# One load queue, wider squares, smaller key-value tiles and fewer last stores in a polysketch-attention and squared-ReLU kernel

## The chip, the cores and the metric

The kernel runs on one core of a Trainium2 chip. The time is the device time in microseconds of one launch. A profiled execution of the same program gives the views that are quoted here. The engines are named as in the profile: PE (TensorE, matrix multiplication; PEld is its weight loading), DVE (VectorE), ACT (ScalarE), POOL (GpSimd) and SP (SyncE, which here only issues DMAs). All DMAs run on the core's 16 DMA engines, through queues that SP, ACT and POOL fill.

## What is computed

Four batches with four heads each have 1088 positions of q, k and v with 32 elements. A feature map takes two 8-element sketches of a row and multiplies them out to 64 features. The attention is linear in these features, and its output (4352 rows of 128) goes through a feed-forward layer whose activation is the square of a ReLU:

```python
def phi(x):
    a = einsum('rd,bhsd->bhsr', S1, x)
    b = einsum('rd,bhsd->bhsr', S2, x)
    return einsum('bhsi,bhsj->bhsij', a, b).reshape(..., 64)
q_p, k_p = phi(q), phi(k)
kv = einsum('bhsf,bhsd->bhfd', k_p, v)
z = sum(k_p, axis=2)
x = (q_p @ kv) / (q_p @ z + 1e-6)      # (4352, 128), heads side by side
out = square(maximum(x @ w_in, 0)) @ w_out     # 128 -> 2048 -> 128
```

Inputs and output are float32. The feed-forward part is computed in bfloat16, the attention in float32.

## The kernel before

**Loads.** `load(b)` (L87) fetches one batch: k as one transfer of 544 KB into `k_in`, v as four transfers of 128 KB (one for each head) and two of 16 KB (the last two of every 34 positions) into `v_in`, and q as one transfer of 544 KB into `q_in`. For batch 0, v is issued by ACT (L102) and k and q by SP, behind two small loads of the sketch matrices into `S12` (L77, L78). SP then issues batches 1 to 3. The framework numbers the hardware-queue DMAs of SP and ACT round eight lanes, and a DMA waits until the one before it in its lane has landed, so at most eight are under way. POOL issues the two weight loads, `w_out` and `w_in` (L121, L119: float32 in memory, converted to bfloat16 on the way), after a copy of one element (L118) that waits for q of batch 0.

**Keys.** `k_stage(b)` (L160) makes the key-value matrix of one batch. DVE transposes k in 32x32 blocks (`block_transpose`, L146) into `kT`. PE projects it onto both sketches (L176). For each of two halves of the positions (`gi` is 0 and 1), ACT copies one sketch out of PSUM into `ka` (L191), DVE multiplies the two sketches out to `kp` in two instructions of 512 columns (L193, one for each half `f` of the features), and v is copied into `v_pad`, which has a column of ones behind each head's 32 columns (L202, L204; by ACT for batch 0, by POOL for the others). PE sums `kp` times `v_pad` over the positions (L215). One matmul takes two heads: 64 columns of `kp` as weights and 66 columns of `v_pad`, so half of the result is the product of one head's keys with the other head's values and is not used. Each half has its own PSUM tile. DVE copies the first half's sums to `kvc` (L226) and adds the second half's with four instructions, one for each head (L230), into `KV`, whose other blocks are zero.

**Queries.** Nine chunks (`ci`): two of 512 columns for each batch, and one of 256 with the last two of every 34 positions of all batches (`qT_rem`). `q_feat` (L254) projects (L266, float32, 128x512), and DVE transposes (L272), multiplies out (L274) and transposes back (L282) to `qp`. `q_out` (L289) multiplies `qp` by `KV` (L304), divides by the denominators on DVE (L318 to L321) and transposes the result on PE (L330), and ACT copies it to `xT` (L336).

**Feed-forward.** `f_stage` (L349) goes over 16 blocks of 128 hidden columns, two at a time: two matmuls into `h_ps` (L358), a ReLU on ACT into `r_sb` (L362, 128x1024), the square on DVE into `g_sb` (L364, 128x1024), and 8 matmuls into `o_ps` (L370). ACT copies `o_ps` to `osb` (L380), and SP stores it: four transfers of 64 KB for a chunk (L383), and for the ninth chunk eight of 16 KB (L389), one for each batch and each of the last two positions.

**Order.** A prologue emits batch 0's keys and chunk 0's queries. After it the feed-forward of one chunk is interleaved with the attention of later ones: each `yield` of `f_stage` advances the attention by some steps (L418 to L432). The Tile framework places each engine's instructions, by a schedule of its own; instructions under `pin` keep the program's order, and `chain` does that for a list of matmuls. Each engine runs its instructions strictly in that order.

Of the kernel before, what the change touches and what calls it, by code (L numbers as in the profile page):

```python
# [21 lines left out]
def kernel(  # L22
# [52 lines left out]

    S12 = consts.tile([2 * r, H, D], F32)
    nc.sync.dma_start(out=S12[:r, 0, :], in_=S1)  # L77
    nc.sync.dma_start(out=S12[r:, 0, :], in_=S2)  # L78

    kin_t, qin_t, vraw, vpad = {}, {}, {}, {}  # L80
    for b in range(B):
        kin_t[b] = kin.tile([128, NJ, D], F32, tag=f"k{b}", name="k_in")
        qin_t[b] = kin.tile([128, NJ, D], F32, tag=f"q{b}", name="q_in")
        vraw[b] = vin.tile([128, H, NLO + 1, D], F32, tag=f"v{b}", name="v_in")
        vpad[b] = vin.tile([128, H, NLO + 1, VW], F32, tag=f"vp{b}", name="v_pad")

    def load(b, veng):  # L87
        nc.sync.dma_start(out=kin_t[b], in_=k[b].rearrange("h (t j) d -> (h t) j d", j=NJ))
        for h in range(H):
            vr = v[b, h].rearrange("(t j) d -> t j d", j=NJ)[:, : 4 * NLO, :]  # L90
            veng.dma_start(
                out=vraw[b][:, h, :NLO, :],
                in_=vr.rearrange("t (i l) d -> i t (l d)", i=4),
            )
        for j2 in range(2):
            veng.dma_start(
# [5 lines left out]
    load(0, nc.scalar)  # L102
    for b in range(1, B):
        load(b, nc.sync)


    ident = consts.tile([128, 128], F32)
    make_identity(nc, ident)
    ident_b = consts.tile([128, 128], BF16)
    nc.vector.tensor_copy(ident_b, ident)  # L110
    for b in range(B):
        nc.gpsimd.memset(vpad[b][:, :, :, D:VW], 1.0)
# [4 lines left out]
    w_in_sb = consts.tile([128, C_TILES, 128], BF16)  # L117
    nc.gpsimd.tensor_copy(w_in_sb[:1, 0, :1], qin_t[0][:1, 0, :1])  # L118
    nc.gpsimd.dma_start(out=w_in_sb, in_=moe_w_in.rearrange("d (ct c) -> d ct c", c=128))  # L119
    w_out_sb = consts.tile([128, C_TILES, 128], BF16)  # L120
    nc.gpsimd.dma_start(out=w_out_sb, in_=moe_w_out.rearrange("(ct c) d -> c ct d", c=128))  # L121

# [23 lines left out]
    def block_transpose(dst, dst_rem, src):  # L146
# [6 lines left out]
        pin(  # L153
            nc.vector.transpose(
                dst_rem, src[:, 4 * NLO :, :].rearrange("p j d -> p (j d)")
            )
        )


    def k_stage(b):  # L160

        kt = kTp.tile([128, S], F32, tag="kT", name="kT")
        block_transpose(kt[:, :1024], kt[:, 1024:], kin_t.pop(b))
# [21 lines left out]
        def features(gi):  # L185
            kk = kks[gi]
            ka = kab_pool.tile([128, 5 * H, r], F32, tag="ka", name="ka")
            kps[gi] = kp = kp_pool.tile([128, 2, 5 * H, 4, r], F32, tag="kp", name="kp")
            for P, g0, g1 in ((128, 0, 4 * H), (64, 4 * H, 5 * H))[: gi + 1]:
                kabv = kk[:P, g0 * 2 * r : g1 * 2 * r].rearrange("p (g x) -> p g x", x=2 * r)  # L190
                nc.scalar.copy(ka[:P, g0:g1], kabv[:, :, :r])  # L191
                for f in range(2):
                    nc.vector.tensor_tensor(  # L193
                        out=kp[:P, f, g0:g1],
                        in0=ka[:P, g0:g1, f * 4 : f * 4 + 4, None].to_broadcast(
                            [P, g1 - g0, 4, r]
                        ),
                        in1=kabv[:, :, None, r:].to_broadcast([P, g1 - g0, 4, r]),
                        op=ALU.mult,
                    )  # L200
# [5 lines left out]
        kvc = kab_pool.tile([128, 2, 2, VW], F32, tag="kvc", name="kvc")  # L206

        def sums(gi):
            kk, kp, seq = kks[gi], kps[gi], seqs[gi]
            kv = kk[:, KV0 : KV0 + 4 * VW].rearrange("p (f x w) -> p f x w", f=2, x=2)  # L210
            for m, P in tiles[gi]:
                for f in range(2):
                    for g in range(2):
                        seq.append(
                            nc.tensor.matmul(  # L215
                                kv[64 * g : 64 * g + 64, f],
                                kp[:P, f, m * H + 2 * g : m * H + 2 * g + 2].rearrange(
                                    "p g i j -> p (g i j)"
                                ),
                                vt[:P, 2 * g : 2 * g + 2, 4 * gi + m, :],  # L220
                                start=(m == 0 and f == 0),
                                stop=(m == len(tiles[gi]) - 1 and f == 1),
                            )
                        )
            if gi == 0:
                nc.vector.tensor_copy(kvc, kv)  # L226
            else:
                for h in range(H):
                    rows = slice(32 * h, 32 * h + 32)
                    nc.vector.tensor_tensor(  # L230
                        out=KV[rows, b, :, h % 2, :],
                        in0=kvc[rows, :, h % 2],
                        in1=kv[rows, :, h % 2],
                        op=ALU.add,
                    )
# [9 lines left out]
    def q_load_stage(b):  # L245
        qt = kTp.tile([128, 1024], F32, tag="qT", name="qT")
        block_transpose(qt, qT_rem[:, b], qin_t.pop(b))
# [101 lines left out]
    def f_stage(ci):  # L349
# [5 lines left out]
        for g2 in range(C_TILES // 2):  # L355
            h_ps = ps_h.tile([128, 2, 512], F32, tag="h", name="h_ps")
            for u in range(2):
                nc.tensor.matmul(  # L358
                    h_ps[:, u, :N], w_in_sb[:, 2 * g2 + u, :], xT[:, :N], start=True, stop=True
                )  # L360
            rt = r_pool.tile([128, 2, 512], BF16, tag="r", name="r_sb")
            nc.scalar.activation(rt[:, :, :N], h_ps[:, :, :N], ACTF.Relu)  # L362
            gt = g_pool.tile([128, 2, 512], BF16, tag="g", name="g_sb")
            nc.vector.tensor_mul(gt[:, :, :N], rt[:, :, :N], rt[:, :, :N])  # L364
            yield
            for u in range(2):
                ct = 2 * g2 + u
# [16 lines left out]
        else:  # L384
            for m in range(2):
                for g in range(4):
                    b, j2 = 2 * m + g // 2, g % 2
                    o = out[b * S : (b + 1) * S].rearrange("(t j) d -> j t d", j=NJ)
                    nc.sync.dma_start(  # L389
                        out=o[32 + j2], in_=osb[32 * g : 32 * (g + 1), m, :]  # L390
# [72 lines left out]
```

## Time and profile before

| what | value |
|---|---|
| time, median of 3 runs | 151.01 us (150.84 to 151.1) |
| profiled execution | 150.13 us, of which 148.3 us are the span of the profile |
| PE, DVE, ACT, POOL busy | 110.3, 108.1, 80.1, 9.1 us |
| k of batch 0 transposed from | 6.30 us |
| last head of v of batch 0 landed | 15.2 us |
| first matmul of the feed-forward | 28.6 us |
| weight loads: issued, us until landed | `w_out` 8.36, 15.1; `w_in` 9.65, 16.2 |
| last instruction of the attention's DVE part (`xb` of chunk 8) | ends at 125.2 us |
| last copy of `o_ps` on ACT (L380) | 142.07 to 142.44 us |

How to read it: a row of the groups names the line, the engine, the operation, and the tile written and read, with its shape and count; then the busy time in us and the mean duration of one in ns; then the idle time of the engine before these instructions and what ended most of it. A float32 matmul leaves two records. A line of the chain is a start in us, a duration in us, and the engine and line. A line of the waits is the instruction that waited, the one that released it, the sum in us, how often, and the longest. A row of a stretch gives its length and then, for PE, PEld, DVE, ACT and POOL in this order, the busy us and the number of instructions, and last the granted clock of PE, the mean number of busy DMA queues per engine, and GB/s. A busy PE is modelled from matmuls in a pipeline, and some matmul records can be missing.

### The profile page before, as it was taken

The page shows a single profiled execution, that of the slowest core. Times are in us where ns is not written, and L with a number is a line of the kernel's source. Part 1 is how long each engine was busy: PE and PEld are TensorE (multiplying, and loading weights), DVE is VectorE, ACT ScalarE, POOL GpSimd, SP SyncE. Part 2 cuts the span into 40 slices and gives each one's busy share as a digit, 9 for nine tenths or more (in the row PEclk, how much of TensorE's full clock was granted, in tenths as well). Part 3 has the DMA queues.
Part 4 walks back from the last instruction along what each step waited for, and adds up shares of the span by engine and source line. Part 5 has one row for each costly group of instructions (what it writes and reads, how often), then busy time and mean ns, then how long its engine had stood idle before and what let it go on. Part 6 is the DMA issues. An engine that isn't in the chain of part 4 may idle for free.

```text
span 148.3 us, 4011 instructions
## 1 busy us (share of the span) xinstructions
PE 110.3 (74%) x1693; PEld 73.7 (50%) x1709; DVE 108.1 (73%) x225; ACT 80.1 (54%) x107; POOL 9.1 (6%) x22
## 2 busy tenths in 40 slices
PE   0050764879997897797988797998897988999820
PEld 0050633437854773584636473764462755566510
DVE  2362476399999859976998986987996987666510
ACT  4000400296664429476294639565837758999810
POOL 2050001104007000000000000000000000000000
PEclk9999999599999689999999999999999999999995
DMA  3949892294452000110002002000200030020201
GB/s 73 358 136 213 160 279 64 102 260 137 121 175 76 23 0 0 39 43 0 0 0 74 1 4 71 4 0 7 66 5 4 0 74 1 0 75 0 73 13 24
DMA packets 8594, 10.22 MB, mean 69 GB/s; under 512 B 4096, under 2 KB 6400, under 8 KB 8576
## 3 DMA queue, kind: packets, MB, share of 16 engines
q1 hardware_dynamic: 5552, 8.36, 19.4%
q0 software_dynamic: 2208, 1.05, 5.4%
q10 hardware_dynamic: 816, 0.56, 1.3%
q8 instruction: 13, 0.21, 0.6%
q14 instruction: 5, 0.04, 0.1%
HBM read 8.78 MB, written 2.23 MB: 74 GB/s over the span
## 4 chain that ended last, share of the span: by engine, by line
DVE 40%; PE 29%; ACT 12%; DMA 8%; issue 5%; ACTq 1%
DVE g_sb L364 14%; ACT r_sb L362 10%; DMA v_in<-in_v_dram 8%; PE kab_ps L215 7%; PE o_ps L370 6%; DVE qf L274 6%; PE pr_ps L266 6%; DVE qp L282 5%; PE nd_ps L304 4%; DVE ab L272 3%; PE h_ps L358 3%; DVE kp L193 3%; DVE xb L321 2%; PE xT_ps L330 2%; DVE KV L230 2%
## 5 line engine op out<-in xcount | busy, mean ns | idle before, releaser
L362 ACT ACTIVATE r_sb<-h_ps 128x1024 bf16<-128x1024 f32 (+1 forms) x72 | 66.9, 984 | 21.0 <-PE pr_ps L266 6.7
L364 DVE TENSOR_TENSOR g_sb<-r_sb 128x1024 bf16<-128x1024 bf16 (+1 forms) x72 | 45.9, 656 | 9.8 <-ACT r_sb L362 9.4
L358 PE MATMUL h_ps<-xT,w_in_sb 128*128 128x512 bf16 (+1 forms) x128 | 37.7, 367 | 8.2 <-ACT r_sb L362 6.3
L370 PE MATMUL o_ps<-w_out_sb,g_sb 128*128 128x128 bf16 x544 | 40.8, 223 | 3.2 <-DVE g_sb L364 1.9
L370 PEld LDWEIGHTS <-g_sb 128*128 128x128 bf16 x544 | 32.3, 99 | 18.3 <-DVE g_sb L364 14.0
L358 PEld LDWEIGHTS <-w_in_sb 128*128 128x128 bf16 x144 | 12.7, 99 | 16.7 <-issue 12.5
L215 PE MATMUL kab_ps<-v_pad,kp 128*64 128x66 f32 (+1 forms) x288 | 11.7, 234 | 7.1 <-ACT v_pad L202 5.8
L193 DVE TENSOR_TENSOR kp<-ka,kab_ps 128x512 f32<-128x512 f32 (+1 forms) x24 | 12.0, 543 | 6.2 <-ACT ka L191 6.2
L215 PEld LDWEIGHTS kab_ps<-v_pad,kp 128*64 128x64 f32 (+1 forms) x288 | 10.3, 145 | 11.1 <-ACT v_pad L202 6.0
L336 ACT COPY xT<-xT_ps 128x512 bf16<-128x512 bf16 (+1 forms) x9 | 5.1, 563 | 17.7 <-PE xT_ps L330 17.7
L304 PEld LDWEIGHTS nd_ps<-KV,qp 64*64 64x64 f32 x544 | 9.7, 142 | 6.3 <-DVE qp L282 4.7
L304 PE MATMUL nd_ps<-KV,qp 64*64 64x66 f32 x544 | 11.3, 231 | 1.4 <-DVE KV L230 1.2
L272 DVE STREAM_TRANSPOSE ab<-pr_ps 128x512 f32<-128x512 f32 (+1 forms) x9 | 6.2, 685 | 8.5 <-PE pr_ps L266 8.5
L274 DVE TENSOR_TENSOR qf<-ab 128x1024 f32<-128x1024 f32 (+1 forms) x9 | 10.7, 1185 | 0.2
L266 PE MATMUL pr_ps<-qT,Wq 128*128 128x512 f32 x16 | 10.2, 721 | 0.7 <-DVE qT L148 0.7
L282 DVE STREAM_TRANSPOSE qp<-qf 128x1024 f32<-128x1024 f32 (+1 forms) x9 | 10.6, 1179 | 0.1
L380 ACT COPY osb<-o_ps 128x512 f32<-128x512 f32 (+1 forms) x9 | 5.1, 570 | 7.4 <-PE o_ps L370 7.4
L176 PE MATMUL kab_ps<-Wk,kT 128*64 128x64 f32 x136 | 6.4, 249 | 3.3 <-DVE Wk L131 3.3
L176 PEld LDWEIGHTS kab_ps<-Wk,kT 128*64 128x64 f32 x136 | 5.5, 159 | 4.6 <-DVE Wk L131 3.4
L191 ACT COPY ka<-kab_ps 128x128 f32<-128x128 f32 (+1 forms) x12 | 2.9, 240 | 8.4 <-PE kab_ps L176 7.0
L321 DVE TENSOR_TENSOR xb<-nd_ps,rec 128x256 bf16<-128x256 f32 (+1 forms) x18 | 6.6, 405 | 0.0
L202 POOL COPY v_pad<-v_in 128x512 f32<-128x512 f32 x6 | 4.5, 779 | 31.7 <-DMA v_in<-in_v_dram 31.7
(39 smaller groups left out, 40.8 us busy)
## 6 DMA issues: line engine op xcount, KB each, us to landing
k_in<-in_k_dram SPq DMA_DIRECT2D x4, 544.0 KB
q_in<-in_q_dram SPq DMA_DIRECT2D x4, 544.0 KB
out_dram<-osb SPq DMA_DIRECT2D x32, 64.0 KB
v_in<-in_v_dram SPq DMA_DIRECT2D x12, 128.0 KB
v_in<-in_v_dram ACTq DMA_DIRECT2D x4, 128.0 KB
w_out_sb<-in_moe_w_out_dram POOLq DMA_DIRECT2D x1, 512.0 KB, 15.1
w_in_sb<-in_moe_w_in_dram POOLq DMA_DIRECT2D x1, 512.0 KB, 16.2
out_dram<-osb SPq DMA_DIRECT2D x8, 16.0 KB
```

Of the source, the lines that this page charges most:

```text
L176: nc.tensor.matmul(kk[64 * c : 64 * c + 64, m * 64 : (m + 1) * 64], kt[:, c0 + 64 * c : c0 + 64 * c + 64], Wk.rearrange("p h x -> p (h x)" ...
L193: nc.vector.tensor_tensor(out=kp[:P, f, g0:g1], in0=ka[:P, g0:g1, f * 4 : f * 4 + 4, None].to_broadcast([P, g1 - g0, 4, r]), in1=kabv[:, : ...
L215: nc.tensor.matmul(kv[64 * g : 64 * g + 64, f], kp[:P, f, m * H + 2 * g : m * H + 2 * g + 2].rearrange("p g i j -> p (g i j)"), vt[:P, 2 * ...
L266: nc.tensor.matmul(pr[:, :N], Wq.rearrange("p h x -> p (h x)"), cols, start=True, stop=True)
L272: nc.vector.transpose(ab[:, :nj].rearrange("p j x -> p (j x)"), pr[:, :N])
L274: nc.vector.tensor_tensor(out=qf[:, :nj], in0=ab[:, :nj, :r, None].to_broadcast([128, nj, r, r]), in1=ab[:, :nj, None, r : 2 * r].to_broad ...
L282: nc.vector.transpose(qp[:, :, :N].rearrange("p f (j t) -> p j f t", t=32), qf[:, :nj].rearrange("p j (f i) k -> p j f (i k)", f=2),)
L304: nc.tensor.matmul(nds[g][64 * c : 64 * c + 64, m * 2 * VW : (m + 1) * 2 * VW], qp[rows, f, c0 : c0 + 64], KV[rows, bs[2 * m + c], f].rear ...
L358: nc.tensor.matmul(h_ps[:, u, :N], w_in_sb[:, 2 * g2 + u, :], xT[:, :N], start=True, stop=True)
L362: nc.scalar.activation(rt[:, :, :N], h_ps[:, :, :N], ACTF.Relu)
L364: nc.vector.tensor_mul(gt[:, :, :N], rt[:, :, :N], rt[:, :, :N])
L370: nc.tensor.matmul(o_ps[:, m, :], gt[:, u, m * 128 : (m + 1) * 128], w_out_sb[:, ct, :], start=(ct == 0 and m == 0), stop=(ct == C_TILES - ...
```

## The change

Four things, in the words of the diff below (helper lines that only move are left out).

- **Loads.** The identity matrix is built first. The sketch matrices are loaded by ACT. All of k, v and q are issued by SP: for each batch k, v, q. POOL's one-element copy ahead of the weight loads waits for the last head of v of batch 0 instead of q of batch 0, and a second one-element copy writes into `k_in` of batch 1 from `w_in`, so that the load of k of batch 1 waits for the weights. In the program as built, SP's order is k, v, q of batch 0; v, q of batch 1; k of batch 2; k of batch 1; then v, q of batch 2 and all of batch 3.
- **Squares.** `r_sb` and `g_sb` hold four blocks instead of two. ACT fills `r_sb` with two ReLUs of 128x1024 as before, DVE squares 128x2048 in one instruction, and 16 matmuls into `o_ps` follow. The pools still have three buffers each.
- **Key-value sums.** `kp` is multiplied out by one instruction of 1024 columns (one of 64x256 for the remainder). A matmul takes one head: 32 columns of `kp` as weights and 33 columns of `v_pad`, into 32 rows of the result. Both halves of the positions add up in the PSUM tile of the first half, and `kvc` and the adds are gone. For batch 0, ACT and DVE copy two heads each into `KV`, in turns (in the built program each of the four waits for the one before). For the other batches ACT copies the whole result to `kvs` (128x66) and POOL copies the four heads (32x66) into `KV`.
- **Last rows.** `qT_rem` is ordered by position first, so that 64 rows of `osb` are one batch. The ninth chunk is stored by four transfers of 64 rows, two issued by SP and two by ACT.

```diff
+    ident = consts.tile([128, 128], F32)
+    make_identity(nc, ident)
     S12 = consts.tile([2 * r, H, D], F32)
-    nc.sync.dma_start(out=S12[:r, 0, :], in_=S1)
-    nc.sync.dma_start(out=S12[r:, 0, :], in_=S2)
+    nc.scalar.dma_start(out=S12[:r, 0, :], in_=S1)
+    nc.scalar.dma_start(out=S12[r:, 0, :], in_=S2)
...
-            veng.dma_start(
+            nc.sync.dma_start(
...
-    load(0, nc.scalar)
+    load(0)
+    for b in range(B):
+        nc.gpsimd.memset(vpad[b][:, :, :, D:VW], 1.0)
+    nc.gpsimd.tensor_copy(w_in_sb[:1, 0, :1], vraw[0][:1, H - 1, 0, :1])
+    nc.gpsimd.dma_start(out=w_in_sb, in_=moe_w_in.rearrange("d (ct c) -> d ct c", c=128))
+    nc.gpsimd.dma_start(out=w_out_sb, in_=moe_w_out.rearrange("(ct c) d -> c ct d", c=128))
+    nc.gpsimd.tensor_copy(kin_t[1][:1, 0, :1], w_in_sb[:1, 0, :1])
     for b in range(1, B):
-        load(b, nc.sync)
+        load(b)
...
-            kps[gi] = kp = kp_pool.tile([128, 2, 5 * H, 4, r], F32, tag="kp", name="kp")
+            kps[gi] = kp = kp_pool.tile([128, 5 * H, r, r], F32, tag="kp", name="kp")
...
-                for f in range(2):
-                    nc.vector.tensor_tensor(
-                        out=kp[:P, f, g0:g1],
...
+                nc.vector.tensor_tensor(
+                    out=kp[:P, g0:g1],
...
         def sums(gi):
-            kk, kp, seq = kks[gi], kps[gi], seqs[gi]
-            kv = kk[:, KV0 : KV0 + 4 * VW].rearrange("p (f x w) -> p f x w", f=2, x=2)
+            kp, seq = kps[gi], seqs[gi]
+            kv = kks[0][:, KV0 : KV0 + 2 * VW].rearrange("p (f w) -> p f w", f=2)
             for m, P in tiles[gi]:
                 for f in range(2):
-                    for g in range(2):
+                    for h in range(H):
                         seq.append(
                             nc.tensor.matmul(
-                                kv[64 * g : 64 * g + 64, f],
...
-                                start=(m == 0 and f == 0),
-                                stop=(m == len(tiles[gi]) - 1 and f == 1),
+                                kv[32 * h : 32 * h + 32, f],
+                                kp[:P, m * H + h, 4 * f : 4 * f + 4].rearrange(
+                                    "p i j -> p (i j)"
+                                ),
+                                vt[:P, h, 4 * gi + m, :],
+                                start=(gi == 0 and m == 0 and f == 0),
+                                stop=(gi == 1 and m == len(tiles[1]) - 1 and f == 1),
                             )
                         )
-            if gi == 0:
-                nc.vector.tensor_copy(kvc, kv)
-            else:
+            if gi:
+                if b:
+                    kvs = kab_pool.tile([128, 2, VW], F32, tag="kvs", name="kvs")
+                    nc.scalar.copy(kvs, kv)
                 for h in range(H):
                     rows = slice(32 * h, 32 * h + 32)
-                    nc.vector.tensor_tensor(
-                        out=KV[rows, b, :, h % 2, :],
...
+                    if b:
+                        eng, src = nc.gpsimd.tensor_copy, kvs
+                    else:
+                        eng, src = (nc.scalar.copy, nc.vector.tensor_copy)[h % 2], kv
+                    eng(KV[rows, b, :, h % 2, :], src[rows])
...
-        for g2 in range(C_TILES // 2):
-            h_ps = ps_h.tile([128, 2, 512], F32, tag="h", name="h_ps")
...
+        for g4 in range(C_TILES // 4):
+            rt = r_pool.tile([128, 4, 512], BF16, tag="r", name="r_sb")
+            gt = g_pool.tile([128, 4, 512], BF16, tag="g", name="g_sb")
+            for g2 in range(2):
+                h_ps = ps_h.tile([128, 2, 512], F32, tag="h", name="h_ps")
...
+                nc.scalar.activation(
+                    rt[:, 2 * g2 : 2 * g2 + 2, :N], h_ps[:, :, :N], ACTF.Relu
                 )
...
+                yield
             nc.vector.tensor_mul(gt[:, :, :N], rt[:, :, :N], rt[:, :, :N])
-            yield
-            for u in range(2):
+            for u in range(4):
...
-                for g in range(4):
-                    b, j2 = 2 * m + g // 2, g % 2
...
+                o = out.rearrange("(b t j) d -> b t j d", b=B, j=NJ)
+                for c, eng in enumerate((nc.sync, nc.scalar)):
+                    eng.dma_start(
+                        out=o[2 * m + c, :, 4 * NLO :, :],
+                        in_=osb[64 * c : 64 * (c + 1), m, :],
                     )
```

## The prediction, as it was put on record before the change was run

> **What bounds the kernel now.** I read the page's busy times and slices first, then the chain that ended last in order of time, then DVE's waits in the long middle, then the single rows. Shares of busy time name two engines:
>
> ```profile
> PE 110.3 (74%) x1693; PEld 73.7 (50%) x1709; DVE 108.1 (73%) x225; ACT 80.1 (54%) x107; POOL 9.1 (6%) x22
> ...
> DVE  2362476399999859976998986987996987666510
> ```
>
> They are averages. The slices (3.7 us each) show three stages: a thin start up to about 28 us, a middle in which DVE is at 8 to 9 tenths, and a thin end. The chain says what the start waits for:
>
> ```profile
> 3.23 11.94 DMA v_in<-in_v_dram
> 15.27 0.63 ACT v_pad L202
> 15.95 2.03 PE kab_ps L215 x32
> 17.97 1.55 PE pr_ps L266 x2
> ...
> 26.37 0.61 PE xT_ps L330 x4
> 26.97 1.83 PE pr_ps L266 x2
> ```
>
> The start waits 12 us for v of batch 0. ACT's copy into `v_pad` waits for it; the second `ka` copy (15.80) stands behind that copy on ACT, and `kp` behind `ka`. From v's arrival (15.2) to the first chunk's transposes (26.4) there are 11.2 us of dependent work. For the middle I asked who DVE waits for between 28 and 122 us:
>
> ```profile
> DVE ab L272 <- PE pr_ps L266: 7.2, 6, 2.5
> DVE g_sb L364 <- ACT r_sb L362: 3.5, 5, 1.4
> ```
>
> and the busy times of two of its stretches (DVE is the third pair of numbers):
>
> ```profile
> 64.00:76.00 12.00, 10.43 (x153) 7.14 (x154) 10.61 (x21) 6.99 (x10) 0.00 (x0) 1.00 0.01 2
> 76.00:88.00 12.00, 10.55 (x206) 6.90 (x206) 10.54 (x21) 7.58 (x9) 0.00 (x0) 1.00 0.10 25
> ```
>
> From 28 to 122 us DVE is busy 82 of 94 us (87%), PE about as long by modelled ends, with ACT 58. DVE bounds the middle, PE is close behind. Prices come from these rows by form and from the end of the SP queue:
>
> ```profile
> L364 DVE TENSOR_TENSOR g_sb<-r_sb 128x1024 bf16<-128x1024 bf16 x64 | 42.6, 685 | 7.9 <-ACT r_sb L362 7.7
> L304 PE MATMUL nd_ps<-KV,qp 64*64 64x66 f32 x544 | 11.3, 231 | 1.4 <-DVE KV L230 1.2
> L215 PE MATMUL kab_ps<-v_pad,kp 128*64 128x66 f32 x256 | 10.2, 235 | 7.1 <-ACT v_pad L202 5.8 <-DVE kp L193 1.3
> L230 DVE TENSOR_TENSOR KV<-kvc,kab_ps 32x66 f32<-32x66 f32 x16 | 3.5, 217 | 0.7 <-PE kab_ps L215 0.5
> L364 DVE TENSOR_TENSOR g_sb<-r_sb 128x512 bf16<-128x512 bf16 x8 | 3.4, 424 | 1.9 <-ACT r_sb L362 1.7
> ```
>
> ```profile
> 142.47 3.56 SPq L389 DMA_DIRECT2D out_dram<-osb  x8
> ```
>
> **Loads.** Now v of batch 0 comes on ACT's queue beside k, q and k of the next batch on SP's, so 0.56 MB in small packets shares the DMA engines with 1.6 MB in large ones. After, SP issues k(0), v(0), q(0), v(1), q(1), k(2); the built program puts k(1) behind these, because it waits for GpSimd's 1x1 copy, which waits for `w_in`. k(0) is issued at 0.74 instead of 1.51 and nothing is ahead of it. A tiny load (S) lands 2.8 us after its issue (0.74 or 1.18 to 4.03), and 0.56 MB at the 366 GB/s of the stretch from 4 to 6 us takes 1.5, so k(0) lands at about 5.0 (before: 6.3). S's two loads (0.38 and 0.28 of issue) move to ACT, where the table load stands between them; the second lands near 5, and `kT`, which DVE now runs first, hides that. v(0)'s six issues move to SP (four of 0.56, two of about 0.7), so SP reaches q(0) at about 5, when k(0) lands. The 816 packets of v's queue took 1.3% of 16 engines' span, 1.9 us if spread evenly; so v(0) lands at about 7, q(0), which waits for k(0)'s landing, at about 9.
>
> From there I add DVE's order in the built program. `kT` 5.05 to 6.3; the S copy, now behind it, 0.24; transpose of S and `Wk` to 7.1; the first half of the projections 1.15, `ka` 0.27, `kp` (as `qf`'s 128x1024, 1.25) to 9.9; q's transposes 1.4 to 11.3; second `kp` to 12.5. PE: first sums 9.9 to 12.2, `pr` 1.55 to 13.9. DVE: `ab` 0.72, the small `kp` 0.4, `qf` and `qp` 1.25 each, to 17.6; four KV copies, handed back and forth between ACT and DVE, 0.8 (they wait for each other; now four adds take 0.9); `nd` 1.1, denominators and `xb` 1.3. Transposes start at 20.9 instead of 26.4: **−5.5 us**. A v(0) that is 1.5 us later costs nothing (ACT needs it at 8.6, PE at 9.9).
>
> What can be late next is `w_in`: the first `h` needs it, and PE reaches `h` at about 23 (after `pr` of chunk 1). Before, the two weight loads were issued at 8.4 and 9.7 and landed after 15.1 and 16.2 us, at 23.5 and 25.9. Their queue's packets take 5.4% of 16 engines' span, 8 us if alone; beside them, from 10.5 on, came some 6.5 us of k, v and q, which sums to 25. After, the first issue is at about 7.3 (behind v's last head) and the second at 8.6, and only some 3.3 us (the end of v(1), q(1), k(2)) stands beside it until `w_in` has landed: about 22. I take no wait. k(1) is then issued at 22.5 and lands near 27; its transpose is due at about 31. On GpSimd the 1x1 copy holds up batch 1's `v_pad` copies until `w_in` is there; the sums need them after 32. v, q, k of batches 2 and 3 follow, needed after 50. SP's 13 issues before k(1) and those behind it wait for nothing else that is late.
>
> **Squares.** From 512 to 1024 columns a square grows by 261 ns, so 2048 take 685 + 2×261 = 1.21 us against 2×0.685. Isolated, a pair saves 0.16 us. Back to back (three in 1.85 us, so 0.583 apart) it saves 0.06. Of the 36 pairs about 25 lie in the middle: 1.5 to 4.1 us; I take 2.0, near the lower end, as DVE has a backlog there. A square now waits for two ACTIVATEs (0.92 apart); the pools hold twice the data, and PE's order has the sums of one group behind the `h` of the next, so I cost that at nothing while DVE has other work. Without this cover one square waits up to 0.9 us.
>
> **Key-value sums.** DVE loses, in each of three batches, four adds (0.92 us together), one `kvc` copy (0.28) and a few fixed costs of `kp` (0.1): 3.9 us. ACT gains three copies of 128x66 (nearest row: `ka` 128x128, 0.27 us); behind each stands an ACTIVATE, whose second matmul is behind the same sums on PE, so it would wait anyway. GpSimd gets 12 copies of 32x66. No row has this shape; alone its 64x128 copy takes 0.29, beside DVE up to 0.75. So KV comes 0.3 + 4×0.3 to 4×0.75 us after the sums, at most 3.3; before, KV(1) was complete at 45.4 and `nd` began at 49.4, so 4 us cover it. DVE pays too: beside the copies at 45.2 to 47.4, `qf` took 1.44 instead of 1.23 and a square 1.09 instead of 0.69. I take 0.6 us for 12 copies, from 0 to 2.4 (0.2 each).
>
> PE: 36 matmuls of 64 columns by 66 become 72 of 32 by 33 per batch, two records each. Now a record follows every 37 ns (40 in 1.49 us) with two column tiles. `nd`, with four tiles, has 64 in 1.17, 18.3 ns. Four tiles of the new shape have no row. At 18.3 the batch takes 2.64 us instead of 2.66: nothing. At half of that, as half the columns could give, −1.3 per batch; at 37, +2.66. I take 18.3, the row with four tiles. The Trainium skill ("TensorE: Matmul & The Clock Gate", section on the 56 ns gap) says that starts of matmuls never come closer than about 25 ns, however few columns; by that 144 records take an estimated 3.6 us, 0.9 more per batch, and the sum below would be 2.8 us later. `nd`'s 18.3 ns contradicts that floor.
>
> DVE's sum in the middle: 2.0 + 3.9 − 0.6 = 5.3 us, of which the 87% share makes 4.6. A batch now takes 27 to 29 us (KV complete at 45.4, 72.8, 101.4), 87% of it DVE's work, 24.4; less 5.3/3 it is 22.6, where PE's stands (16×0.88 for `h` and `o`, 2.0 `pr`, 1.25 projections, 2.66 sums, 2.4 `nd`, 0.8 transposes), so PE takes over part of the bound: **−4 us**, from +1.5 (the second rival) to −7 (4.1 + 3.9, times 0.87).
>
> **Last rows and tail.** SP's last eight issues take 0.445 us each. After, two queues issue two each: the last issue starts 0.45 instead of 3.1 us after `osb`, −2.7; at the 1.14 us that ACT's issue took at 0.74 it is −2.0. I take **−2.5**. The last square is 0.68 instead of 0.42, followed by 8 matmuls instead of 4: **+0.5**.
>
> **Sum.** The profiled execution has a span of 148.3 and took 150.13 us, 0.9 under the median of 151.01. −5.5 −4 −2.5 +0.5 = −11.5: a span of 136.8, a time of 138.6, and on the median's scale 139.5.
>
> **Rivals.**
> - *The weights are late.* `w_in` lands at 25.5 as before. For: both queues go through the same 16 engines, and stragglers of the weights ran until 25 us. Against: k(1) no longer competes. First squares then start 2.5 us later: 142.
> - *DVE's gain does not reach the end.* Coarser squares make DVE wait for ACT and PE, whose 7.2 us of `pr` waits stay. For: PE is at 82 of 94 us already. The middle gives 0, or loses 1.5: 143.5 to 145.
> - *Everything in DVE counts*, at 0.16 us a pair and with PE's sums at half: 136.
> - *Slower: column tiles that do not overlap.* Place: the sums, 576 records. For: no row shows 128x32, and PE has little slack. At 37 ns a record the sums take 21.3 instead of 10.7 us, which alone eats the gain (150); if nothing overlaps, 74 ns, 42.6 us and a time of 171. It decides from about 38 ns on. Against: two tiles and four overlap fully in the rows above.
> - *The change does not do what it says*: v(0) still lands after 13 us because one queue's packets queue behind k. Then −2 instead of −5.5: 143. The queue's 290 to 366 GB/s speak against it.
>
> **Numbers.** Forecast (137 to 141.5) 0.50; late weights 0.14; lost middle 0.15; more from DVE 0.08; v(0) still late 0.04; slower 0.07; 0.02 is left for no change. A measurement of this kernel can tell about 0.2%, 0.3 us, from no change. So faster 0.91, same 0.02, slower 0.07. Range: 135 (all of DVE's terms, PE's sums at half) to 145.5 (middle lost).
>
> **What would show it.** `kT` at 5 us, second `kp` before 13, first `xT_ps` at 21, first `h` at 23. Squares of 1.21 us. Sums per batch of 2.6 us, and no DVE work on KV after batch 0. `nd` waiting for `qp`, not for GpSimd. Two issues on SP and two on ACT at the end, and under 4 us after `osb`. I am wrong if `h` waits for `w_in`, if the sums' records are over 25 ns apart, or if DVE's idle time in the middle grows by more than 5 us.

## The result and the profile after

The changed kernel takes 145.43 us (median of 4 runs, 145.27 to 145.95), the kernel before 151.06 beside it; the ratio is 0.963, with an interval from 0.9605 to 0.9662. The gain is 5.6 us; 11.5 had been forecast. Medians and ratios here and below are of the fast runs: a run more than 1.5% above the fastest of its kernel is left out as slow. The time lies just inside the range on record (135 to 145.5), far from the forecast (139.5, with 137 to 141.5 as its likeliest part).

The busy times and DVE's slices of the changed kernel (3.6 us each) answer to those shown of before:

```profile
PE 106.3 (74%) x1981; PEld 71.8 (50%) x1997; DVE 101.1 (70%) x159; ACT 81.0 (56%) x112; POOL 17.0 (12%) x35
...
DVE  2534753679899399886995997799579575655530
```

DVE works 7 us less (108.1 before), yet the span shrinks only from 148.3 to 143.8 us: DVE idles 42.7 us instead of 40.2. What DVE waited for between 28 and 122 us (sum, times, longest) says where:

```profile
DVE g_sb L366 <- ACT r_sb L362: 6.4, 9, 1.2
DVE ab L266 <- PE pr_ps L260: 4.4, 3, 1.9
DVE den L312 <- PE nd_ps L298: 3.4, 4, 1.3
DVE kp L191 <- ACT ka L190: 1.1, 3, 0.4
```

The waits for `pr` are shorter (7.2 before), those of squares for ReLUs nearly twice as long (3.5 before), and `den` has joined them. The same two stretches as before:

```profile
64.00:76.00 12.00, 10.43 (x222) 7.12 (x223) 10.54 (x11) 8.53 (x11) 4.33 (x7) 1.00 0.09 23
76.00:88.00 12.00, 9.63 (x169) 6.37 (x162) 10.08 (x21) 7.49 (x10) 0.00 (x0) 1.00 0.06 15
```

Neither PE nor DVE is fuller than before. The groups, by form:

```profile
L366 DVE TENSOR_TENSOR g_sb<-r_sb 128x2048 bf16<-128x2048 bf16 x32 | 38.9, 1221 | 11.4 <-ACT r_sb L362 11.3
...
L209 PE MATMUL kab_ps<-v_pad,kp 128*32 128x33 f32 x512 | 7.0, 210 | 3.4 <-ACT v_pad L198 3.1
...
L229 POOL COPY KV<-kvs 32x66 f32<-32x66 f32 x12 | 6.6, 552 | 55.8 <-ACT kvs L222 55.3
```

A square takes the 1.21 us forecast; before, DVE idled 7.9 us ahead of its 64 squares, now 11.4 ahead of 32. For the start, the waits for DMAs up to 30 us:

```profile
POOL w_in_sb L110 <- DMA v_in<-in_v_dram: 9.6, 1, 9.6
...
DVE qT L149 <- DMA q_in<-in_q_dram: 3.5, 1, 3.5
...
ACT v_pad L198 <- DMA v_in<-in_v_dram: 3.2, 1, 3.2
...
PE h_ps L355 <- DMA w_in_sb<-in_moe_w_in_dram: 0.7, 1, 0.7
```

v, q and `w_in` are all waited for. And the end, from the timeline:

```profile
139.40 0.37 ACT L381 COPY osb<-o_ps 128x256 f32<-128x256 f32 x1 [1.44 <-PE o_ps L371]
139.80 1.28 SPq L389 DMA_DIRECT2D out_dram<-osb  x2
139.80 1.29 ACTq L389 DMA_DIRECT2D out_dram<-osb  x2
```

The two profiled executions (150.13 and 145.95 us) can be cut into four stretches that add up to their spans:

| stretch | before | after | difference | forecast |
|---|---|---|---|---|
| to the first ReLU | 29.50 | 27.94 | −1.6 | −5.5 |
| first ReLU to the end of the last | 111.61 | 110.02 | −1.6 | −4.0 |
| to the last copy of `o_ps` | 0.96 | 1.44 | +0.5 | +0.5 |
| from there to the end | 6.23 | 4.40 | −1.8 | −2.5 |

So two steps are short: the start by 3.9 us and the middle by 2.4, and the last stores by 0.7.

### The profile page after: what moved, and what is told of

Same layout as the page of the kernel before. It is cut to its first block, busy times and chain, and to the rows that moved or that the text cites. A ratio compares the mean times of both kernels' runs of the same rounds, so it can differ in the third digit from the quotient of the medians.

```text
span 143.8 us, 4505 instructions
## 1 busy us (share of the span) xinstructions
PE 106.3 (74%) x1981; PEld 71.8 (50%) x1997; DVE 101.1 (70%) x159; ACT 81.0 (56%) x112; POOL 17.0 (12%) x35
## 4 chain that ended last, share of the span: by engine, by line
DVE 26%; PE 23%; DMA 16%; issue 14%; ACT 11%; POOL 4%; SPq 2%; another core or an unknown queue 1%; ACTq 0%; POOLq 0%
DMA v_in<-in_v_dram 16%; DVE g_sb L366 11%; PE o_ps L371 10%; ACT r_sb L362 9%; PE h_ps L355 4%; DVE qf L268 4%; DVE qp L276 4%; DVE ab L266 3%; POOL KV L229 3%; PE nd_ps L298 3%; SPq L95 2%; DVE kT L149 2%; PE pr_ps L260 2%; PE kab_ps L209 2%; PE kab_ps L175 1%
## 5 line engine op out<-in xcount | busy, mean ns | idle before, releaser
L366 DVE TENSOR_TENSOR g_sb<-r_sb 128x2048 bf16<-128x2048 bf16 (+1 forms) x36 | 41.6, 1162 | 13.7 <-ACT r_sb L362 13.6
L355 PE MATMUL h_ps<-xT,w_in_sb 128*128 128x512 bf16 (+1 forms) x128 | 38.5, 376 | 9.8 <-ACT r_sb L362 8.1
L371 PE MATMUL o_ps<-w_out_sb,g_sb 128*128 128x128 bf16 x544 | 36.3, 219 | 4.5 <-DVE g_sb L366 3.8
L355 PEld LDWEIGHTS <-w_in_sb 128*128 128x128 bf16 x144 | 12.7, 99 | 22.6 <-issue 18.5
L298 PE MATMUL nd_ps<-KV,qp 64*64 64x66 f32 x544 | 12.5, 234 | 3.4 <-DVE KV L229 2.1
L298 PEld LDWEIGHTS nd_ps<-KV,qp 64*64 64x64 f32 x544 | 10.6, 143 | 7.7 <-DVE KV L229 2.3
L229 POOL COPY KV<-kvs 32x66 f32<-32x66 f32 x12 | 6.6, 552 | 55.8 <-ACT kvs L222 55.3
L191 DVE TENSOR_TENSOR kp<-ka,kab_ps 128x1024 f32<-128x1024 f32 (+1 forms) x12 | 11.2, 941 | 2.4 <-ACT ka L190 2.4
L268 DVE TENSOR_TENSOR qf<-ab 128x1024 f32<-128x1024 f32 (+1 forms) x9 | 11.1, 1228 | 0.2
L209 PE MATMUL kab_ps<-v_pad,kp 128*32 128x33 f32 (+1 forms) x576 | 8.4, 210 | 3.5 <-ACT v_pad L198 3.1
L209 PEld LDWEIGHTS kab_ps<-v_pad,kp 128*32 128x32 f32 (+1 forms) x576 | 7.1, 121 | 7.2 <-ACT v_pad L198 4.8
L149 DVE STREAM_TRANSPOSE qT<-q_in 128x1024 f32<-128x1024 f32 x4 | 4.9, 1234 | 3.5 <-DMA q_in<-in_q_dram 3.5
```

What stands on the lines that cost most here:

```text
L191: nc.vector.tensor_tensor(out=kp[:P, g0:g1], in0=ka[:P, g0:g1, :, None].to_broadcast([P, g1 - g0, r, r]), in1=kabv[:, :, None, r:].to_broa ...
L209: nc.tensor.matmul(kv[32 * h : 32 * h + 32, f], kp[:P, m * H + h, 4 * f : 4 * f + 4].rearrange("p i j -> p (i j)"), vt[:P, h, 4 * gi + m, ...
L229: eng(KV[rows, b, :, h % 2, :], src[rows])
L268: nc.vector.tensor_tensor(out=qf[:, :nj], in0=ab[:, :nj, :r, None].to_broadcast([128, nj, r, r]), in1=ab[:, :nj, None, r : 2 * r].to_broad ...
L298: nc.tensor.matmul(nds[g][64 * c : 64 * c + 64, m * 2 * VW : (m + 1) * 2 * VW], qp[rows, f, c0 : c0 + 64], KV[rows, bs[2 * m + c], f].rear ...
L355: nc.tensor.matmul(h_ps[:, u, :N], w_in_sb[:, 4 * g4 + 2 * g2 + u, :], xT[:, :N], start=True, stop=True,)
```

## The experiments

**Theory.** (1) v's transfers run on a few DMA engines only, so v, then q behind it, then the weights are late. (2) A square that waits for two ReLUs gives its saving back in waits. **Rivals.** Small packets, or one queue behind k, are slow in any layout; the new sums or GpSimd's copies cost more than forecast; the squares do gain and something else takes it.

### Each part alone

Four kernels: the kernel before with one part of the change each (the four parts are those of the change's section, with its diff).

> The kernel before with the change's loads alone. Theory A (v's transfers are the slow part of the start, however they are queued): v of batch 0 lands near 11 us as in the changed kernel, w_in near 26.8, and the time falls by the 1.6 us by which the first ReLU came earlier there (29.5 to 27.9): 149.4, between 148.5 and 150. Rival B (the loads give what the prediction said, and other parts lose it): 145.5, -5.5.

> The kernel before with 2048-wide squares alone. Theory A (DVE's saving in the middle does not reach the end, because the order of the feed-forward units on ACT and PE sets the pace): -0.5, between -1.5 and +0.5. Rival B (the prediction's terms, 2.0 times 0.87 in the middle and +0.5 in the tail): -1.2. Rival C (waiting for two ReLUs costs more than the fixed cost of 36 squares): +1 or more, with DVE waiting longer for ACT than 9.4 us.

> The kernel before with the new key-value sums alone. Prediction's terms: 3.9 - 0.6 on DVE, times 0.87: -2.9. Theory A (order, not DVE, sets the pace): between 0 and -1.5. Rival C (GpSimd's copies are late and hold up PE and DVE): 0 or more, with PE's numerator matmuls waiting for GpSimd by 1 us or more in a batch.

> The kernel before with the four last stores and the new order of the remainder columns alone. In the changed kernel the two issues of each queue took 1.28 us together, and the end came 4.0 us after the last copy began to be stored instead of 5.8: -1.8, between -1.4 and -2.2. The prediction had -2.5.

Measured, against 151.22 for before: loads 147.58 (ratio 0.976, 0.970 to 0.982), squares 154.12 (1.018, 1.011 to 1.025), sums 149.01 (0.986, 0.981 to 0.991), last rows 149.50 (0.989, 0.984 to 0.995). The loads alone bring 3.6 us, outside both expectations (1.6 and 5.5). Their profiled execution is the slow one of the four runs (149.45), so where the rest comes from stays open. The wide squares alone are 2.9 us slower, as in rival C. The sums alone gain, so slow column tiles are out: in the changed kernel 64 records of them take

```profile
40.67 0.77 PE L209 MATMUL kab_ps<-v_pad,kp 128*32 128x33 f32 x64
```

12 ns each, against the 18.3 taken. The last rows bring 1.7. Together the four come to −4.7, the whole to −5.6; each of the four is known to about 1 us, so this does not say whether they act on each other.

### v over more engines, the squares, the pace, GpSimd's copies

All four are the changed kernel with one edit. `spread` cuts v by 32-partition group:

```diff
-        for h in range(H):
-            vr = v[b, h].rearrange("(t j) d -> t j d", j=NJ)[:, : 4 * NLO, :]
+        for i in range(4):
+            vr = v[b].rearrange("h (t j) d -> t h j d", j=NJ)[:, :, NLO * i : NLO * (i + 1), :]
...
-                out=vraw[b][:, h, :NLO, :],
-                in_=vr.rearrange("t (i l) d -> i t (l d)", i=4),
+                out=vraw[b][32 * i : 32 * (i + 1), :, :NLO, :],
+                in_=vr.rearrange("t h l d -> t h (l d)"),
```

`no_squares` has `f_stage` as before; `pace` has `(unit + 6) / 74.0` for `66.0`; `kv_no_pool` copies `KV` for all batches as for batch 0.

> The changed kernel with only v's four large loads of a batch cut another way: by 32-partition group (32 rows by four heads) instead of by head (four groups by 32 rows). Number, bytes and packet size (1024 bytes) stay; the slowest dimension of the source goes from 4 to 32. The copy ahead of the weights still waits for the last of the four. Theory (each transfer of v runs on four of the 16 engines, since its slowest dimension is 4, and this holds back q and the weights): v(0) lands at about 7 to 8 instead of 11.1 us, the second kp at 12.5 instead of 14.0, the first xT_ps at 21.5 to 22.5 instead of 23.8, the weights 2 us earlier; time 142.5 to 144 against 145.4 for the whole change. Rival (small packets, or one queue behind k, are slow in any layout): v(0) stays at 11 and the time within 0.5 us of 145.4.

> The changed kernel with the squares back at 1024 columns; loads, sums and last rows as changed. Theory (a 2048-wide square ties two ReLUs and four h together, so that DVE and ACT wait for each other in the middle): 142.5 to 144.5, DVE's wait for ACT r_sb back from 13.6 to about 9, PE waiting less for g_sb. Rival (the terms of the prediction: squares save 2.0 us of DVE, 0.06 each): 146.6 to 147.4. Third reading (squares alone cost 2.9, but the other parts' spare DVE time hides it): within 0.5 us of 145.4.

> The changed kernel with one constant: the attention's steps are spread over more of the feed-forward's units (74 in the divisor instead of 66), so that attention advances less per unit. In the whole change the attention's last xb moved 5.7 us earlier but the last ReLU only 3.1. Theory (attention is emitted ahead of the feed-forward, and takes PE and DVE from it): 143.5 to 145, with fewer ReLUs left after the last xT (19 now). Rival (the middle is bound by busy time, whichever goes first): 145 to 146.

> The changed kernel with the key-value copies of batches 1 to 3 made by ACT and DVE in turns out of PSUM, as for batch 0, instead of ACT's one copy and GpSimd's four. Theory (GpSimd's copies cost little: nd waited 0.76 us once, in batch 1; DVE gains 3 times 2 copies of 0.2): within 0.8 us of 145.4 either way. Rival (GpSimd's slow copies, 552 ns in the mean, hold nd and so the attention, or slow DVE down beside them): 143.5 to 144.5.

Measured, beside a kernel before of 150.19: `spread` 143.23 (ratio 0.952, 0.941 to 0.963), `no_squares` 144.98 (0.966, 0.957 to 0.976), `pace` 146.72 (0.976, 0.967 to 0.985), `kv_no_pool` 147.03 (0.979, 0.972 to 0.987).

- `spread` gained, but less of the start moved than expected: v at 9.05, q still at 12.7, the first `xT_ps` at 23.4 (23.8 in the whole change). So it is q that the start waited for. Its built program had also moved `w_out`'s load from 11.30 to 1.55 us, ahead of GpSimd's wait. Two edits in one; they are taken apart below.
- `no_squares` is within the scatter of the whole change: the squares bring nothing in it. The theory's gain (142.5 to 144.5) did not come, and neither did its sign, shorter waits of squares for ReLUs; more on this below.
- `pace` was expected to gain and lost 1.3: the attention's chain must not be held back.
- `kv_no_pool` lost 1.6, against both expectations. Two in-order queues that hand copies to each other wait; between 28 and 120 us:

```profile
DVE KV L223 <- ACT KV L223: 4.2, 5, 1.5
...
ACT KV L223 <- PE kab_ps L209: 2.5, 2, 1.5
```

So GpSimd's route is a gain, although its copies are slow (0.55 us each in the mean): in the changed kernel `nd` waited for them once, 0.8 us.

### q ahead of v, spread without wide squares, the old sums

> The whole change again, as the yardstick for the runs beside it: 145.0 to 145.9.

> The run with v's loads spread by 32-partition group, and in each batch k, q, v instead of k, v, q. With v spread, v(0) landed at 9.1 but q(0) still at 12.7, and the first xT_ps came at 23.4. Theory (from q(0) on, the prologue is one chain of 10.7 us, so that the load that lands last, q(0), sets the first xT_ps): q(0) lands at 7.5 to 9, v(0) at 9.5 to 11, the first xT_ps at 20.5 to 22, time 1 to 2 us less than with v, q order (143.6). Rival (the middle takes up an early start, since DVE and PE are full there): first xT_ps as early, time within 0.5 us of 143.6.

> v's loads spread by 32-partition group and squares of 1024 columns; sums and last rows as changed. Theory (in the whole change the 2048-wide squares bring nothing: DVE's shorter time is given back in waits for two ReLUs): within 0.7 us of the run with spread v alone (143.6). Rival (the prediction's 1.7 us of gain from the squares is there, but hidden by late loads): 144.6 to 145.5.

> The changed kernel with the key-value sums as before (64 columns by 66, kvc and four adds on DVE); loads, squares and last rows as changed. Theory (the new sums are worth about what they brought alone, 2.2 us): 147 to 148.5 against 145.4 for the whole change. Rival (DVE's gain from the sums doesn't reach the end once the squares are wide): 145 to 146.

`qfirst` is `spread` with q's line moved from behind v to behind k; `no_sums` has `k_stage` as before. Measured: the whole change again 145.43 (ratio 0.967, 0.962 to 0.971), `qfirst` 141.96 (0.942, 0.938 to 0.946), `spread_ns` 143.09 (0.952, 0.948 to 0.956), `no_sums` 149.00 (0.990, 0.986 to 0.993). With q ahead, q lands at 7.0 and v at 11.1; the first `xT_ps` starts at 20.6 and the first `h` at 22.8. The new sums are worth 3.6 us in the whole, against 2.2 alone.

### v's cut and w_out's place, apart

`spread_held` is `spread`, but a second copy of one element, into `w_out_sb`, makes `w_out` wait for v as in the whole change; `w_out_early` is the whole change with `w_out`'s load moved ahead of the wait:

```diff
+    nc.gpsimd.dma_start(out=w_out_sb, in_=moe_w_out.rearrange("(ct c) d -> c ct d", c=128))
     nc.gpsimd.tensor_copy(w_in_sb[:1, 0, :1], vraw[0][:1, H - 1, 0, :1])
```

> v's loads spread by 32-partition group as before, but w_out's load waits for v of batch 0, as in the whole change (a second one-element copy on GpSimd). Theory (v's cut makes v, and q behind it, late; w_out's early load took the DMA engines from them in the run with v spread): v(0) lands at 6.5 to 8 (11.1 in the whole change, 9.1 with w_out early), q(0) at 8.5 to 10.5 (12.7 in both), first xT_ps at 21 to 22, time 141.5 to 143.5. Rival (one queue in this order is slow whatever the cut, and w_out's early load was what helped): v(0) after 9, q(0) after 12, time 144.5 to 146.

> The whole change with w_out's load issued at about 1.5 us, ahead of the wait for v; v is cut as in the change (four groups of partitions by 32 rows). Theory (v's transfers use few engines, and w_out now shares them): v(0) at 11 to 14, q(0) at 12.7 to 15, w_in 1 to 4 us earlier than 26.8; time 144.5 to 147. Rival (w_out's place is what brought the 2 us of the run with v spread): v(0) and q(0) as there, 143 to 144.

Measured: `spread_held` 142.04 (four runs, 141.54 to 143.63; ratio 0.944, 0.938 to 0.950), `w_out_early` 147.59 (0.977, 0.972 to 0.982). In `spread_held` GpSimd's one-element copy, which waits for v's last head, the first `xT_ps` and the first `h` (the new line moves later ones on by one):

```profile
6.93 0.19 POOL L110 CAST w_in_sb<-v_in 1x1 bf16<-1x1 f32 x1 [5.33 <-DMA v_in<-in_v_dram]
...
21.09 0.61 PE L325 MATMUL xT_ps<-ident_b,xb 128*128 128x128 bf16 x4 [1.27 <-DVE xb L316]
...
23.30 0.63 PE L356 MATMUL h_ps<-xT,w_in_sb 128*128 128x512 bf16 x1
```

v lands at 6.9, q at 9.2, and `h` starts at 23.3. In `w_out_early` v lands at 13.3 and q at 15.4, and it is 2.2 us slower than the whole change, although `w_in` lands at 21.3, 5.4 us earlier. So the gain belongs to v's cut. `w_out`'s early place harms with v on few engines and brought nothing in `spread` (143.23, with an interval that overlaps this one). The theory's part 1 stands; both rivals to it fell. The events on the loads' semaphores in the packed traces show it directly: the load of v's last head ends in four pieces in the changed kernel (10.5 to 11.1 us) and in 16 in `spread_held` (6.2 to 6.8). And q of the changed kernel, in 16 pieces, has 12 of them done between 9.5 and 10.1 us but the last four between 11.9 and 12.7, as if four engines had v to finish first. The stretches show it too: the last three columns are the granted clock, the mean number of busy DMA queues per engine and GB/s. The changed kernel, then `spread_held`:

```profile
5.00:7.00 2.00, 0.69 (x9) 0.61 (x11) 1.57 (x6) 0.00 (x0) 0.00 (x0) 1.00 0.43 111
```

```profile
5.00:7.00 2.00, 0.30 (x3) 0.22 (x3) 1.83 (x6) 0.00 (x0) 0.07 (x1) 1.00 1.00 241
```

0.43 at 111 GB/s while v and q are awaited: more than half of the engines' time is unused. Spread, the same loads keep one queue busy on every engine in the mean. The kernel before had such a stretch while v was awaited, and I passed over it:

```profile
9.00:11.00 2.00, 1.15 (x20) 0.96 (x17) 1.57 (x3) 0.27 (x1) 1.21 (x2) 1.00 0.43 109
```

### The wide squares

> The changed kernel (145.4) with each 2048-wide square made as two 1024-wide ones in the same place; the tiles of four blocks and the groups of 16 matmuls into o_ps stay. DVE has some 0.15 us times 36 = 5 us more to do. Theory (a square that waits for two ReLUs gives the saving back): 144.5 to 146, as with 1024-wide squares and groups of 8 (145.0). Rival (the groups of 16 matmuls order PE and ACT coarsely, and the wide square itself is a gain): 147.5 to 149.

> The changed kernel (145.4) with one more DVE instruction behind each of the 32 squares of the first eight chunks: a square of 128 columns again (the same values into the same place), an estimated 0.23 us each from the rows of 512 and 1024 columns, 7.3 us of DVE in all. The prediction's reading (87% of DVE's time in the middle counts): 150.5 to 152. Rival (DVE has become slack that waits for PE and ACT): under 147.5. In between, DVE's share is what the slope says.

> v spread, k, q, v order, and squares of 1024 columns; sums and last rows as changed. Theory (wide squares bring nothing once the new sums are in): within 0.7 us of the same with wide squares (142.0). Rival (with the start mended, DVE bounds more and the wide squares pay): 142.9 to 144.

> The run before with 60 in the divisor of the attention's pace instead of 66. With 74, the whole change was 1.3 us slower. Theory (the attention's chain through DVE is the longer one, so the earlier it goes the better): 0.5 to 1.5 us faster than with 66. Rival (66 is near the best, since the ReLUs left for the end are ACT's 0.92 us each): 0 to 1.5 us slower.

```diff
-            nc.vector.tensor_mul(gt[:, :, :N], rt[:, :, :N], rt[:, :, :N])
+            for g2 in (0, 2):
+                nc.vector.tensor_mul(
+                    gt[:, g2 : g2 + 2, :N], rt[:, g2 : g2 + 2, :N], rt[:, g2 : g2 + 2, :N]
+                )
```

That is `sq_split`. `dve_more` instead adds `nc.vector.tensor_mul(gt[:, 0, :128], rt[:, 0, :128], rt[:, 0, :128])` behind the square. `qfirst_ns` joins `qfirst` and `no_squares`; `qfirst_ns_ahead` has 60 for 66 as well.

Measured: `sq_split` 144.55 (0.961, 0.956 to 0.965), `dve_more` 151.41 (1.006, 1.003 to 1.009), `qfirst_ns` 140.94 (0.938, 0.934 to 0.942), `qfirst_ns_ahead` 139.97 (0.932, 0.927 to 0.937). With q ahead, narrow squares are 1.0 us faster than wide ones, where at most 0.7 had been expected. The added instructions of `dve_more`:

```profile
L368 DVE TENSOR_TENSOR g_sb<-r_sb 128x128 bf16<-128x128 bf16 x32 | 7.8, 246 | 0.4
```

7.8 us more of DVE cost 6.0 us, 0.77 each. But the added instruction also stands between a square and its `o_ps` matmuls, which wait for it. PE's waits ahead of these matmuls between 28 and 137 us, first in the changed kernel, then here:

```profile
PE o_ps L371 <- DVE g_sb L366: 2.7, 7, 0.6
```

```profile
PE o_ps L373 <- DVE g_sb L368: 7.5, 12, 1.4
```

So DVE work in this place counts; that DVE work in any place does is not shown by this run. The split squares, by contrast,

```profile
L367 DVE TENSOR_TENSOR g_sb<-r_sb 128x1024 bf16<-128x1024 bf16 x64 | 43.0, 691 | 12.9 <-ACT r_sb L362 12.5
```

take 4.7 us more of DVE than the wide ones (43.0 + 3.4 against 38.9 + 2.8), and the kernel is no slower for it (0.9 less). This table has for each profiled execution the stretch from the first ReLU's start to the last one's end, and in it DVE's busy time and the rest:

| run | time | first ReLU | stretch | DVE busy | DVE idle |
|---|---|---|---|---|---|
| before | 151.1 | 29.5 | 111.6 | 94.4 | 17.2 |
| whole change | 145.4 | 27.9 | 110.0 | 87.0 | 23.0 |
| whole change again | 145.4 | 27.3 | 109.6 | 87.0 | 22.6 |
| `squares_only` | 154.1 | 30.0 | 113.0 | 89.9 | 23.1 |
| `sums_only` | 149.0 | 30.4 | 109.4 | 90.7 | 18.6 |
| `rows_only` | 149.5 | 31.7 | 110.1 | 93.8 | 16.4 |
| `no_sums` | 149.0 | 28.0 | 113.5 | 88.1 | 25.4 |
| `no_squares` | 145.0 | 27.5 | 109.6 | 89.8 | 19.8 |
| `sq_split` | 144.6 | 28.5 | 109.6 | 89.6 | 20.0 |
| `spread` | 143.2 | 26.7 | 109.5 | 87.3 | 22.2 |
| `spread_held` | 142.0 | 24.4 | 110.0 | 87.3 | 22.7 |
| `w_out_early` | 147.6 | 29.1 | 110.1 | 87.3 | 22.8 |
| `qfirst` | 142.0 | 23.9 | 110.3 | 87.3 | 23.0 |
| `qfirst_ns` | 140.9 | 24.2 | 109.4 | 90.7 | 18.6 |
| `qfirst_ns_ahead` | 140.0 | 23.9 | 108.6 | 90.8 | 17.8 |

Two things stand in it. With the same middle the stretch is 109.5 to 110.3 whether it begins at 23.9 or 29.1: the start's gain reaches the end. And wide squares save 2.6 to 4.5 us of DVE's busy time and add 3.0 to 5.9 us of idle time, in every pair of rows (whole and `no_squares`, whole and `sq_split`, `qfirst` and `qfirst_ns`, `squares_only` and before), so that the stretch gets no shorter. `sq_split` keeps the groups of 16 matmuls and has the idle time of narrow squares, so it is the wide instruction, not the coarser groups.

Where the idle time lies is another matter, and I had it wrong. The waits of `no_squares` between 28 and 122 us, to be held against those of the changed kernel at the top:

```profile
DVE g_sb L358 <- ACT r_sb L356: 8.4, 13, 1.5
DVE den L312 <- PE nd_ps L298: 0.4, 2, 0.2
```

Ahead of squares DVE waits no less with narrow ones (8.4 us against 6.4; over the whole stretch 13.5 against 13.7). What is longer with wide ones in the changed kernel is the wait of `den` for `nd`: 3.4 us in four waits, against 0.4. Before one of the four, at 48.1, `nd` had waited for GpSimd; before each of the other three PE ran 16 matmuls of `o_ps`, which had waited 0.3 us for a wide square, ahead of the last `nd`. In `squares_only` the waits ahead of squares did grow. So that wide squares bring nothing in the whole is shown; the way their saving is lost is read from a few places. Here is one, early in the changed kernel's middle:

```profile
32.03 1.22 DVE L366 TENSOR_TENSOR g_sb<-r_sb 128x2048 bf16<-128x2048 bf16 x1 [0.90 <-ACT r_sb L362]
...
33.17 1.24 DVE L149 STREAM_TRANSPOSE qT<-q_in 128x1024 f32<-128x1024 f32 x1
...
33.31 1.07 PE L371 MATMUL o_ps<-w_out_sb,g_sb 128*128 128x128 bf16 x16 [0.57 <-DVE g_sb L366]
...
34.22 0.38 PE L355 MATMUL h_ps<-xT,w_in_sb 128*128 128x512 bf16 x1
...
34.85 1.02 ACT L362 ACTIVATE r_sb<-h_ps 128x1024 bf16<-128x1024 f32 x1 [2.85 <-remote]
```

DVE waits 0.90 us for the second ReLU, although the transpose of q behind it needs nothing that is late (that q landed at 23.3). PE waits for the square, and the next `h` stands behind its 16 matmuls, so ACT idles 2.85 us before the ReLU of that `h` (the view can't name the releaser, "remote"), and the next square is late in turn. Each engine takes its instructions in order, so here one wait passes round all three. The table also shows where wide squares cost time: with the old sums they lengthen the stretch (113.0 and 113.5 us against 111.6), with the new ones hardly (109.5 to 110.3 against 109.4 to 109.6). So the new sums are worth more beside wide squares than alone; why that is stays open. One reserve: every edit lets the framework place other instructions anew, and part of a difference between two programs can be that. `rows_only` leaves loads, sums and squares as they were, and yet its first ReLU comes 2.2 us later and its stretch is 1.5 us shorter than before.

`qfirst_ns_ahead` beats both kernels: 139.97 us. `spread_held` with narrow squares and the earlier pace was not run.

## Why the prediction was wrong

- **v's landing: the step that failed most.** "The 816 packets of v's queue took 1.3% of 16 engines' span, 1.9 us if spread evenly; so v(0) lands at about 7". They are not spread evenly: v landed at 11.1, on four engines, and q behind it at 12.7 (forecast 9). DVE's transposes of q began at 12.7, with the second `kp` behind them, and the first `xT_ps` came 2.9 us late, at 23.8. The weight loads, issued from 11.3 instead of 7.3, brought `w_in` at 26.8 instead of 22, and the first ReLU lost 3.9 us in all. Cut so that they spread, v lands at 6.9, and 3.5 us of this come back at the first ReLU, 3.4 in the time. The Trainium skill ("DMA: Bandwidth & Descriptors", section "Why a DMA increments its semaphore by 16 and not by 1") says that a transfer uses the largest number of engines, at most 16, that divides the slowest dimension of both sides. The slowest dimension of a v load's source is the 4 of `i`, which by that rule gives four engines; the four pieces in which it lands agree, and so do the 16 with 32 rows in that place.
- **The rest of the prologue was right in its sum, with some luck in its terms.** In `spread_held` v and q land as forecast (6.9 and 9.2), and `xT_ps` at 21.1 and `h` at 23.3 stand beside 20.9 and 23. But the second `kp` ended at 10.8, not 12.5, since DVE ran it ahead of q's transposes, and `nd` took 2.0 us instead of 1.1.
- **The squares: "I cost that at nothing while DVE has other work".** DVE is busy in the middle, but in order: work that stands behind a waiting instruction covers nothing. The forecast took 2.0 us of DVE as gain, 1.7 in time. DVE's time did fall (2.8 us in the whole change), and as much idle time came: no gain in the whole, a loss of 2.9 us alone. By the waits above, the idle time in the whole lies less ahead of the squares than ahead of `den`, behind PE.
- **The sums were about right.** 2.9 us forecast (3.3 of DVE at 87%), 2.2 measured alone and 3.6 in the whole. The slow tiles that could have made the change slower were refuted by 12 ns a record (a float32 matmul leaves two). So was, for these tiles, the floor of about 25 ns that the Trainium skill states ("TensorE: Matmul & The Clock Gate", section on the 56 ns gap).
- **The middle as a whole.** The text named its own test: "if DVE's idle time in the middle grows by more than 5 us". From the first ReLU to the last it grew by 5.8 (by 4.5 between 28 and 122 us, the stretch that the text had used), and DVE's busy time fell by 7.4, more than the 5.3 of the sum. So saved DVE time did not come out at the 87% used: the stretch got 1.6 us shorter for 7.4 saved, 2.0 for 4.6 in `no_squares` and 2.3 for 3.7 in `sums_only`. Added DVE work cost 0.77 us per us in the one place tried, but there PE waits for it.
- **Last rows.** −1.8 (−1.7 alone) instead of −2.5: an issue of 64 rows takes 0.64 us, where the 0.445 of 32 rows was used, and from the end of the last issue to the end of the span there are 2.7 us instead of 2.3.
- **The rivals.** Two of them happened at once, each in part: v late (11.1, not after 13) and the middle's gain lost. The range was built from one case at a time, and that the time still lies 0.07 us inside it is luck.

## What to carry to other kernels

Before a load's landing time is worked out from its bytes, look at the busy DMA share while it is awaited: a share stuck at 0.4 with a load outstanding meant that few engines worked; here a slowest dimension of 4 gave four engines and one of 32 gave 16. A wider instruction that must wait for two producers, and that others wait for in turn, can give its saving back as idle time; compare idle plus busy, not busy alone. Where a start's gain and a middle's gain are forecast, cut both traces at the same event (here the first and the last ReLU): it shows at once which of them failed.

## What the runs showed of the hardware that was not expected

- Matmuls of 128x32 weights by 33 columns on four column tiles leave a record every 12 ns.
- Four issues of v on SP took 2.70 us with 4 by 32 rows and 1.84 us with 32 by 4, for the same bytes and packets. That this is the shape is not shown: issues of the same shape further on in the changed kernel took 0.56 to 1.52 us each.
- GpSimd's copy of 32x66 took 0.23 us at the median and 1.65 at the longest, beside a busy DVE.
- The float32 `pr` in the start of the changed kernel and of `spread` takes 2.02 to 2.04 us and one in the middle 1.02, although the granted clock stood at 1.00 in the changed kernel's start and at 0.50 in that of `spread` (20 to 24 us): the clock column did not tell the two apart.
